# A DFT-and-GLU kernel: another order for the opening's loads, stores and first three steps

## Chip, cores, metric

The kernel runs on one core of one Trainium2 chip. Its time is the device time of one launch in microseconds (us); the median of three runs is compared. The profile is a hardware trace of one execution. The engines are TensorE (PE, with its weight loads as PEld), VectorE (DVE), ScalarE (ACT), GpSimd (POOL) and SyncE (SP), which here only issues DMAs. ScalarE and GpSimd issue some DMAs too, each on a queue of its own.

## What is computed

```python
X = np.fft.fft(x, axis=1)            # x: 8 x 3008 x 256, float32
X = np.fft.fft(X, axis=2)
h = X.real.reshape(24064, 256) @ w_in    # w_in: 256 x 2048
g = h * np.cos(h)
out = g @ w_out                      # w_out: 2048 x 256, out: 24064 x 256
```

All in float32. The output has 24,064 rows of 256.

## The kernel before

*The transform.* The sequence length is 3008 = 47 x 64. For each of the 8 batches, `first_half` multiplies the 47-point part: x lies in `xs[0]` and `xs[1]` (columns 0 to 15 and 16 to 31 of the 64, each with its mirror column), is folded along the feature axis by `fold` (sum and difference of mirrored features) and goes through TensorE in eight chunks of four columns to `z`. The result is evicted by ScalarE to tiles `zs`, stored to DRAM (`store_z`), and read back in another order (`load_z`). It is stored in two parts: "near" (far = 0, four of the 24 frequency rows, needed for the first group) and "far". `second_half` then multiplies the 64-point part with the table `BJ`, four rows at a time, which gives a group's `pq`. There are six groups (`NG`) of 225 or 256 columns in each batch.

*The weights.* The DFT over the feature axis is folded into w_in: `fold_weights(e, n)` multiplies a quarter n (512 columns) of w_in by the cosine (e = 0) or sine (e = 1) table into `WC` or `WS`. One row of the result, the norm row, is copied by VectorE to `nrow`, sent to DRAM (`send_wn`) and read back as columns `wn` (`take_wn`). `combine_w2(f0, f1)` makes four combinations of w_out's blocks on VectorE, four subtractions or additions for each call.

*The steps.* The body is a pipeline of 384 steps, eight for each group: `mm1` (two pairs of matmuls into PSUM tile `H`), a scaled copy `act_e`, `dve_h`, rounding (`act_round`, `dve_frac`), `act_sin`, `dve_g`, sums `dve_s`, and seven matmuls `mm2` three steps later (`LAG` = 3). Before `mm1`, `H` is filled: `seed` does it on ScalarE from the norm (tile `nb`) and `wn`; for step 0 `fill_first` and `seed_first` do it with a memset and two matmuls whose operand has one row. There are three `H` tiles.

*What sets the order.* The order is written out by hand (`tc.manual_schedule()`): every engine and every DMA queue takes its instructions in the order in which the Python code records them. DMA completions use eight counters shared by the SP and ScalarE queues; a DMA waits until the transfer that last used its counter has landed. The main loop over t records step t's parts; `opening` and `early` hang extra work on the steps 0 to 22, and `todo`, `aside` and `between` hang the next batch's transform on them.

*The opening.* LCS (DFT tables) and the first quarter of w_in come first on SP. Then the first half of x: its front part on SP in pieces of at most 2 KB, its mirrored part on ScalarE's queue, one mirror column (three small loads) on GpSimd's. The second half is all on SP. The second quarter of w_in and the first BJ columns follow. `chunk(c)` is fold(0, c, 0) and fold(0, c, 1). Chunk c + 1 is folded while TensorE multiplies chunk c:

```python
    for c in range(NCH):
        if c + 1 < NCH:
            chunk(c + 1)
        first_half(0, c)
        store_z(0, c, 0)
        if c == 3:
            load_w(2)
            load_w2(0, 4)
            send_wn(0)
    load_z(0, 0)
```

After it stand the near load of z, quarter 1's folds, one fold of quarter 2, six of the eight w2 blocks' combinations, the far z stores of the chunks 0 to 3 and `second_half(0, 0)`. Steps 0 to 2 go through the general loop, with `early` adding the remaining weight folds: one of quarter 2 in step 0, the two of quarter 3 in steps 1 and 2.

Of the kernel before, what the change touches and what calls it, by code (L numbers as in the profile page):

```python
# [18 lines left out]
ND = 256  # L19
NDFF = 2048  # L20
N2 = 47
NJ = 24
# [4 lines left out]
IP = 4  # L27
NCH = NI // IP
XP = 4 * IP
NG = 6  # L30
# [12 lines left out]
def _consts():  # L43
# [21 lines left out]
    LO0 = stack(np.sin(th), z, z, np.sin(thh))  # L65
    L = np.concatenate([LE, LO, LE0, LO0], axis=1)
    rows = np.zeros((128, 256))
    for side in range(2):
# [65 lines left out]
def kernel(  # L134
# [10 lines left out]
    LCS_dr = nc.inline_tensor(  # L145
        np.concatenate([L_np[:, 0:256], CS_np[0:128], CS_np[128:256]], axis=1), name="dft_L"
    )
    V_dr = nc.inline_tensor(np.ascontiguousarray(L_np[:, 256:640]), name="dft_V")
    ident_dr = nc.inline_tensor(np.eye(128, dtype=np.float32), name="ident")
# [38 lines left out]
    def load_x(b, p):  # L188
        xv = xs[p][0 : 16 * STEP].rearrange("(e g) c -> e g c", g=STEP)
        i0 = XP * p  # L190
        back = nc.sync if p else nc.scalar

        def load(queue, g, c0, c1, cols, **more):
            for m in range(3):
                k = 15 if m == 2 else 16
                queue.dma_start(
                    out=xv[0:k, g + m, ND * c0 : ND * c1].rearrange("e (i d) -> e i d", d=ND),
                    in_=x_r[b, 16 * m : 16 * m + k, cols],
                    **more,
                )  # L200

        load(nc.sync, 0, 0, XP, slice(i0, i0 + XP), max_dma_last_dim=2048)
        c0 = 0 if p else 1
        load(back, 3, c0, XP, slice(64 - i0 - c0, 64 - i0 - XP, -1))
        if p == 0:
            load(nc.gpsimd, 3, 0, 1, slice(32, 33))

    LCS = cpool.tile([128, 768], FP, tag="LCS", name="LCS")
    L = LCS[:, 0:256]
    CS = [LCS[:, 256 + 256 * i : 512 + 256 * i] for i in range(2)]  # L210
    wr = [
        spool.tile([128, n], FP, tag=tag, bufs=k, name="wr")
        for tag, n, k in (("mr", 1792, 1), ("cb", 1792, 1), ("r", 1024, 4), ("r", 1024, 4))
    ]
    BJ = cpool.tile([128, NJ * 128], FP, tag="BJ", name="BJ")
    w2 = cpool.tile([128, 16 * ND], FP, tag="w2", name="w2")

    def load_w(q):
        nc.sync.dma_start(
            out=wr[q][:, 0:1024].rearrange("p (i f) -> p i f", i=2),  # L220
            in_=moe_w_in.rearrange("(i p) f -> p i f", p=128)[:, :, 512 * q : 512 * q + 512],
        )

# [23 lines left out]
    nc.gpsimd.memset(xs[0][:, 2048:4096], 0.0)  # L247
    nc.vector.memset(VX[:, 0:512], 1.0)
    nc.vector.memset(ones, 1.0)
    nc.vector.memset(mask, 1.0)  # L250
    nc.vector.memset(mask[0:1], 0.0)
    nc.vector.memset(xs[1], 0.0)
    load_x(0, 0)
    for xf in xf0:
        nc.gpsimd.memset(xf[64:128], 0.0)
        nc.gpsimd.memset(xf[0:64, 512:1024:128], 0.0)
    load_x(0, 1)
    load_w(1)
    load_bj(0, 512)
    WC = cpool.tile([128, NDFF], FP, tag="WC", name="WC")  # L260
# [4 lines left out]
    xz = cpool.tile([128, ND], FP, tag="xz", name="xz")  # L265
    xs2 = [cpool.tile([128, 2 * ND], FP, tag=f"xs{e}", name="xs") for e in range(2)]
    xf1 = [cpool.tile([128, 512], FP, tag=f"xf{i}", name="xf") for i in range(2)]
# [14 lines left out]
    def fold(b, c, e):  # L282
# [3 lines left out]
        if e == 0:  # L286
            nc.gpsimd.tensor_copy(out=fv[:, 0, :, 0], in_=xv[:, :, 0])
        nc.vector.tensor_tensor(
# [120 lines left out]
    def first_half(b, c):  # L409

        if b:
            return first_half_later(b, c)
        if c % 4 == 0:
            middle(b, c // 4)
        fv = xf0[c % 2].rearrange("r (e c) -> r e c", e=2)
        LE, LO, LE0, LO0 = (L[:, 64 * q : 64 * q + 64] for q in range(4))
        pz = psum("pz", "M")
        a = 128 if c == 0 else 0
        for e, (w, w0) in enumerate(((LE, LE0), (LO, LO0))):
            rows = slice(64 * e, 64 * e + 64)  # L420
            if a:
                nc.tensor.matmul(
                    pz[rows, 0:128], lhsT=w0, rhs=fv[:, e, 0:128], start=True, stop=True
                )
# [12 lines left out]
    def store_z(b, c, far):  # L437
# [15 lines left out]
        for e in range(2):  # L453
            queue = nc.scalar if not far and (e or c > 3) else nc.sync
            queue.dma_start(
# [12 lines left out]
    def second_half(b, g):  # L468
# [16 lines left out]
        if g == 0:  # L485
            nc.scalar.copy(
                out=pv[:, :, 0:192].rearrange("d e (q k) -> d e q k", k=64), in_=bv[:, :, 1:4, :]
            )
            nc.scalar.copy(out=pv[:, :, 192:225], in_=bv[:, :, 0, 0:33])
        else:  # L490
# [10 lines left out]
    def spread_norm():  # L501
# [3 lines left out]
        nc.tensor.matmul(pn[:, 0:T], lhsT=ones, rhs=pq[0:1, T : 2 * T], start=True, stop=True)  # L505
        nc.scalar.copy(out=nb[:, 0:T], in_=pn[:, 0:T])

# [4 lines left out]
    def transform(b):  # L512
        t0 = (b - 1) * NG * 8

        def at(o, *call):
            todo.setdefault(t0 + o, []).append(call)

# [23 lines left out]
    def fold_weights(e, n, tag="M"):  # L541
        W = WS if e else WC
        pw = psum("pw", tag)
        for i in range(2):
            nc.tensor.matmul(  # L545
                pw,
                lhsT=CS[i][:, 128 * e : 128 * e + 128],
                rhs=wr[n][:, 512 * i : 512 * i + 512],
                start=(i == 0),
# [74 lines left out]
    def seed_first(s):  # L624
        T = s.T
        s.pq, s.nb = ready[s.b, s.grp]
        for u in range(2):
            nc.tensor.matmul(
                s.H[:, u * T : u * T + T],
                lhsT=nrow[0][0:1, 128 * u : 128 * u + 128],  # L630
                rhs=s.pq[0:1, T : 2 * T],
# [223 lines left out]

    keep_busy(1, "H", 512)
    fold_weights(1, 0, "H")
    fold_weights(0, 0, "H")
    chunk(0)
    for c in range(NCH):  # L860
        if c + 1 < NCH:
            chunk(c + 1)
        first_half(0, c)
        store_z(0, c, 0)
        if c == 3:
            load_w(2)
            load_w2(0, 4)
            send_wn(0)
    load_z(0, 0)
    load_w2(4, 8)  # L870
    take_wn(0)
    load_w(3)
    fill_first(steps[0])
    fold_weights(1, 1)
    fold_weights(0, 1)
    send_wn(1)
    load_bj(512, 1024)
    combine_w2(0, 2)
    combine_w2(2, 4)
    fold_weights(1, 2)  # L880
    take_wn(1)
    send_wn(2)
    combine_w2(4, 6)
    for c in range(NCH // 2):
        store_z(0, c, 1)
    second_half(0, 0)
    seed_first(steps[0])
    early = {0: (0, 2), 1: (1, 3), 2: (0, 3)}
    opening = {
        0: ((combine_w2, 6, 8), (take_wn, 2)) + tuple((store_z, 0, c, 1) for c in (4, 5)),  # L890
        1: ((send_wn, 3),) + tuple((store_z, 0, c, 1) for c in (6, 7)) + ((take_wn, 3),),
        2: ((clear_later,), (load_z, 0, 1), (load_bj, 1024, NJ * 128), (load_v,)),
        5: ((second_half, 0, 1),),
# [3 lines left out]
        22: ((second_half, 0, 5),),  # L897
    }
    n = len(steps)
    for b in range(1, NB):  # L900
        transform(b)

    def step(t, last=None):
# [11 lines left out]

    for t in range(n + LAG + 1):
        cur, prev, old, done = step(t), step(t - 1), step(t - 2), step(t - LAG)
        if cur:
            mm1(cur, 0)
            act_e(cur)  # L920
            if t == 0:
                spread_norm()
            if t in early:
                fold_weights(*early[t])
# [22 lines left out]
        for call in between.pop(t, ()):  # L947
            call[0](*call[1:])
        if done and t <= n:
            dve_s(done, 2)  # L950
# [56 lines left out]
```

## Time and profile before

| what | value |
|---|---|
| median of three runs (lowest, highest) | 1952.91 us (1952.51, 1953.36) |
| the profiled execution, its own time | 1953.48 us |
| its span, first to last instruction | 1951.7 us |
| granted TensorE clock, mean over the span | 0.994 |
| busy: PE, DVE, ACT, POOL | 1924.2, 1781.7, 1530.5, 396.0 us |
| moved by DMA | 89.32 MB, mean 46 GB/s |
| step 0's first matmul (L628) begins | 43.21 us |
| step 3's first matmul (L642) begins | 61.75 us |
| step 8's first matmul (L642) begins | 84.15 us |

A line such as "L642 PE MATMUL H<-pq,WC 128x225 x4" names the line of the code, the engine, the operation, the tile written and the tiles read, the size, and how many there were. One float32 matmul shows as two MATMUL records, so a pair of matmuls is x4. "[8.33 <-DMA w]" behind an instruction means that its engine had stood idle for 8.33 us, and that a DMA into tile w ended that. In the chain of waits every row is a start, a length and what the chain went through there; a DMA row ends when the data is in. "SPq" and "ACTq" are DMA issues. The granted clock is a share of TensorE's full clock.

### The profile page before, as it was taken

The page shows a single profiled execution, that of the slowest core. Times are in us where ns is not written, and L with a number is a line of the kernel's source. Part 1 is how long each engine was busy: PE and PEld are TensorE (multiplying, and loading weights), DVE is VectorE, ACT ScalarE, POOL GpSimd, SP SyncE. Part 2 cuts the span into 40 slices and gives each one's busy share as a digit, 9 for nine tenths or more (in the row PEclk, how much of TensorE's full clock was granted, in tenths as well). Part 3 has the DMA queues.
Part 4 walks back from the last instruction along what each step waited for, and adds up shares of the span by engine and source line. Part 5 has one row for each costly group of instructions (what it writes and reads, how often), then busy time and mean ns, then how long its engine had stood idle before and what let it go on. Part 6 is the DMA issues. An engine that isn't in the chain of part 4 may idle for free.

```text
span 1951.7 us, 30532 instructions
## 1 busy us (share of the span) xinstructions
PE 1924.2 (99%) x9524; PEld 1691.9 (87%) x9524; DVE 1781.7 (91%) x3343; ACT 1530.5 (78%) x2881; POOL 396.0 (20%) x464
## 2 busy tenths in 40 slices
PE   6999999999999999999999999999999999999998
PEld 3888889888998889988899888988889888898887
DVE  4889999999999998999989999899999999999998
ACT  2788878887788788887878888788877888788775
POOL 5022202222022211222112221122211222111101
PEclk8999999999999999999999999999999999999999
DMA  7321231012200122001211122110231100110000
GB/s 202 93 56 38 49 91 26 19 39 67 65 24 23 41 77 51 25 24 47 81 38 27 26 53 76 33 31 24 52 85 29 25 22 24 54 28 10 12 22 22
DMA packets 159969, 89.32 MB, mean 46 GB/s; under 512 B 108948, under 2 KB 153931, under 8 KB 157339
## 3 DMA queue, kind: packets, MB, share of 16 engines
q1 hardware_dynamic: 157135, 84.65, 16.7%
q0 software_dynamic: 1280, 1.68, 0.4%
q8 instruction: 76, 1.25, 0.3%
q10 hardware_dynamic: 1392, 1.05, 0.2%
q14 instruction: 86, 0.70, 0.1%
HBM read 50.04 MB, written 37.28 MB: 45 GB/s over the span
## 4 chain that ended last, share of the span: by engine, by line
PE 96%; DMA 1%; DVE 1%; issue 0%; ACT 0%; SPq 0%; ACTq 0%; POOL 0%; DVEq 0%; POOLq 0%
PE M L732 58%; PE H L642 34%; PE pb L475 2%; PE pz L382 2%; DMA zd<-zs 1%; DMA xp<-in_x_dram 1%; PE pz L342 0%; PE pw L545 0%; PE pz L425 0%; SPq L839 0%; PE M L382 0%; DVE r L687 0%; DMA z<-zd 0%; PE pz L370 0%; DVE S L698 0%
## 5 line engine op out<-in xcount | busy, mean ns | idle before, releaser
L732 PE MATMUL M<-S,VX 128*128 128x256 f32 (+1 forms) x2304 | 612.4, 375 | 0.0
L732 PEld LDWEIGHTS M<-S,VX 128*128 128x128 f32 x2304 | 437.8, 190 | 49.8
L673 ACT ACTIVATE r<-H 128x512 f32<-128x512 f32 (+1 forms) x384 | 226.1, 589 | 264.1 <-DVE h L658 263.3
L683 ACT ACTIVATE r<-r 128x1024 f32<-128x1024 f32 (+1 forms) x384 | 394.7, 1028 | 21.2 <-DVE r L677 16.1
L642 PE MATMUL H<-pq,WC 128*128 128x256 f32 (+1 forms) x1536 | 394.7, 379 | 1.9 <-ACT H L612 1.9
L642 PE MATMUL H<-pq,WS 128*128 128x256 f32 (+1 forms) x1536 | 387.8, 375 | 0.6 <-ACT ew L653 0.5
L732 PE MATMUL M<-r,w 128*128 128x256 f32 (+1 forms) x1536 | 387.7, 375 | 0.0
L612 ACT ACTIVATE H<-nb,wn 128x256 f32<-128x256 f32 (+1 forms) x766 | 363.0, 474 | 13.9
L658 DVE TENSOR_TENSOR h<-ew,H 128x512 f32<-128x512 f32 (+1 forms) x384 | 258.8, 674 | 103.3 <-PE H L642 72.4
L642 PEld LDWEIGHTS H<-pq,WC 128*128 128x128 f32 x1536 | 283.6, 190 | 52.5 <-ACT r L673 15.8
L732 PEld LDWEIGHTS M<-r,w 128*128 128x128 f32 x1536 | 300.3, 196 | 27.2
L642 PEld LDWEIGHTS H<-pq,WS 128*128 128x128 f32 x1536 | 291.7, 190 | 36.0 <-ACT ew L653 1.8
L677 DVE SCALAR_TENSOR_TENSOR r<-r,H 128x512 f32<-128x512 f32 (+1 forms) x384 | 258.6, 674 | 29.7 <-ACT r L673 13.0
L653 ACT ACTIVATE ew<-H 128x512 f32<-128x512 f32 (+1 forms) x384 | 225.7, 588 | 55.0 <-PE H L642 46.3
L784 POOL TENSOR_TENSOR cb<-cb,mr 128x256 f32<-128x256 f32 (+3 forms) x188 | 158.3, 852 | 517.8 <-DVE S L708 483.4
L698 DVE TENSOR_TENSOR S<-r 128x512 f32<-128x512 f32 (+1 forms) x384 | 258.8, 674 | 0.1
L677 DVE SCALAR_TENSOR_TENSOR r<-r,h 128x512 f32<-128x512 f32 (+1 forms) x384 | 258.4, 673 | 0.0
L687 DVE SCALAR_TENSOR_TENSOR r<-h,r 128x512 f32<-128x512 f32 (+1 forms) x384 | 258.0, 672 | 0.0
L687 DVE SCALAR_TENSOR_TENSOR r<-H,r 128x512 f32<-128x512 f32 (+1 forms) x384 | 255.9, 666 | 0.9 <-ACT r L683 0.5
L673 ACT ACTIVATE r<-h 128x512 f32<-128x512 f32 (+1 forms) x384 | 236.0, 615 | 0.0
L301 POOL TENSOR_TENSOR xs<-xp 113x512 f32<-113x512 f32 x112 | 143.1, 1278 | 440.9 <-DVE S L708 440.9
L732 PE MATMUL M<-S,w 128*128 128x256 f32 (+1 forms) x768 | 225.6, 375 | 0.6 <-DVE S L708 0.6
(94 smaller groups left out, 1579.7 us busy)
## 6 DMA issues: line engine op xcount, KB each, us to landing
out_dram<-ob SPq DMA_DIRECT2D x728, 32.0 KB
xp<-in_x_dram SPq DMA_DIRECT2D x250, 56.0 KB
z<-zd SPq DMA_DIRECT2D x8, 1280.0 KB
zd<-zs SPq DMA_DIRECT2D x224, 40.0 KB
nb<-nd SPq DMA_DIRECT2D x40, 128.0 KB
zd<-zs SPq DMA_DIRECT2D x224, 8.0 KB
xp<-in_x_dram SPq DMA_DIRECT2D x52, 48.0 KB
wr<-in_moe_w_in_dram SPq DMA_DIRECT2D x4, 512.0 KB
```

The lines of the kernel that those rows point to most:

```text
L301: return nc.gpsimd.tensor_tensor(out=xs2[e][0:XL], in0=xv[:, 0], in1=xv[:, 1], op=ALU.subtract if e else ALU.add,)
L612: nc.scalar.activation(out=s.H[:, u * T : u * T + T], in_=s.nb[:, 0:T], func=AF.Copy, bias=0.25, scale=wn[:, f : f + 1],)
L642: nc.tensor.matmul(s.H[:, u * T : u * T + T], lhsT=W[:, 128 * f : 128 * f + 128], rhs=s.pq[:, e * T : e * T + T], start=False, stop=True, ...
L653: nc.scalar.mul(out=s.ew[:, 0 : 2 * s.T], in_=s.H[:, 0 : 2 * s.T], mul=2.0)
L658: nc.vector.tensor_tensor(out=s.h[:, 0 : 2 * T].rearrange("p (u t) -> p u t", u=2)[:, :, ::-1], in0=s.ew[:, 0 : 2 * T].rearrange("p (u t) ...
L673: nc.scalar.activation(out=r, in_=h, func=AF.Copy, bias=BIG, scale=1.0)
L677: nc.vector.scalar_tensor_tensor(out=r, in0=r, scalar=-BIG, in1=h, op0=ALU.add, op1=ALU.subtract)
L683: nc.scalar.activation(out=r, in_=r, func=AF.Sin, bias=0.0, scale=SIN_SCALE)
L687: nc.vector.scalar_tensor_tensor(out=r, in0=h, scalar=-0.25, in1=r, op0=ALU.add, op1=ALU.mult)
L698: return nc.vector.tensor_tensor(out=sv[:, 0:2], in0=gv[:, 2:3].to_broadcast([128, 2, T]), in1=gv[:, 0:4:3], op=ALU.subtract,)
L732: nc.tensor.matmul(acc[key][m // 2][:, 256 * (m % 2) : 256 * (m % 2) + T], lhsT=w, rhs=a, start=first, stop=s.fp == 7, skip_group_check=True,)
L784: return nc.gpsimd.tensor_tensor(out=o, in0=a, in1=b, op=ALU.subtract if less else ALU.add)
```

## The change

It touches the opening only; the loop is the same from step 3 on, apart from what hangs on the steps 3 and 4.

- x of batch 0 is all on SP, first half and then second half, in pieces of 1 KB. The three small mirror loads stay with GpSimd. The clearing of `xs[1]` is split between VectorE and GpSimd.
- The loads of w_in are cut into two for each quarter; quarters 1 and 2, the first two w2 blocks and the first BJ columns are recorded right behind x, ahead of the z stores. Quarter 3 goes to the tiles `xs2`.
- The chunks go 0, 1, 2, 3, 7, 4, 5, 6. Chunk 7 (`DIRECT`) is not folded: TensorE takes x as it is, with two matmuls for each half, the second on reversed columns, and a table of negated sines (`NLO`) is added to LCS.
- The near z stores of the chunks 0 to 3 go to GpSimd's queue, one of each of the chunks 4 and 7 to SP, the rest to ScalarE. The column copy of `fold` goes from GpSimd to ScalarE. Two small copies (`edge` in `second_half`, `nb` in `spread_norm`) go from ScalarE to VectorE.
- The w2 blocks come in four loads, two of them right behind the near load of z. All far z stores and the far load are recorded ahead of step 0.
- Steps 0 to 2 are written out by hand in an order of their own, with step 1 seeded by matmuls as well; the folds of quarter 3 move to steps 3 and 4 and use another PSUM tile, and the combinations of the last two w2 blocks move there too.

```diff
-    L = np.concatenate([LE, LO, LE0, LO0], axis=1)
+    L = np.concatenate([LE, LO, LE0, LO0, -LO], axis=1)
...
-        load(nc.sync, 0, 0, XP, slice(i0, i0 + XP), max_dma_last_dim=2048)
+        load(nc.sync, 0, 0, XP, slice(i0, i0 + XP), max_dma_last_dim=1024)
         c0 = 0 if p else 1
-        load(back, 3, c0, XP, slice(64 - i0 - c0, 64 - i0 - XP, -1))
+        load(nc.sync, 3, c0, XP, slice(64 - i0 - c0, 64 - i0 - XP, -1))
...
+    xs2 = [cpool.tile([128, 2 * ND], FP, tag=f"xs{e}", name="xs") for e in range(2)]
+    wr.append(xs2)
...
+        for i in range(2):
+            nc.sync.dma_start(
+                out=wr[q][i],
+                in_=moe_w_in[128 * i : 128 * i + 128, 512 * q : 512 * q + 512],
+            )
...
+    nc.vector.memset(xs[1][:, 0:2048], 0.0)
+    nc.gpsimd.memset(xs[1][:, 2048:4096], 0.0)
...
-    nc.vector.memset(xs[1], 0.0)
...
     load_x(0, 1)
+    load_bj(0, 512)
     load_w(1)
-    load_bj(0, 512)
+    load_w2(0, 2)
+    load_w(2)
...
-            nc.gpsimd.tensor_copy(out=fv[:, 0, :, 0], in_=xv[:, :, 0])
+            nc.scalar.copy(out=fv[:, 0, :, 0], in_=xv[:, :, 0])
...
+            if c == DIRECT:
...
+                nc.tensor.matmul(
+                    pv[rows], lhsT=w[0:XR], rhs=xv[:, :, 0:128], start=True, stop=False
+                )
+                nc.tensor.matmul(
+                    pv[rows, :, 1:128],
+                    lhsT=(NLO if e else LE)[0:XR],
+                    rhs=xv[:, :, 255:128:-1],
+                    start=False,
+                    stop=True,
+                )
+                continue
...
-            queue = nc.scalar if not far and (e or c > 3) else nc.sync
+            queue = nc.sync if far or (e == 0 and c in (4, 7)) else nc.scalar
+            if c < 4 and not far:
+                queue = nc.gpsimd
...
-            nc.scalar.copy(out=pv[:, :, 192:225], in_=bv[:, :, 0, 0:33])
+            edge = nc.scalar.copy if b else nc.vector.tensor_copy
+            edge(out=pv[:, :, 192:225], in_=bv[:, :, 0, 0:33])
...
-        nc.scalar.copy(out=nb[:, 0:T], in_=pn[:, 0:T])
+        nc.vector.tensor_copy(out=nb[:, 0:T], in_=pn[:, 0:T])
...
-    keep_busy(1, "H", 512)
+    keep_busy(2, "H", 512)
...
+    order = [c for c in range(NCH) if c < 4] + [DIRECT] + [c for c in range(4, NCH) if c != DIRECT]
...
+    clear_later()
+    send_wn(0)
+    for s in steps[0:2]:
+        fill_first(s)
+    combine_w2(0, 2)
     fold_weights(1, 1)
     fold_weights(0, 1)
     send_wn(1)
+    load_z(0, 0)
     fold_weights(1, 2)
+    load_w2(2, 4)
+    load_w2(4, 6)
     take_wn(1)
     send_wn(2)
+    take_wn(0)
+    load_w(3)
+    load_w2(6, 8)
     for c in range(NCH // 2):
         store_z(0, c, 1)
+    take_wn(2)
+    for c in range(NCH // 2, NCH):
+        store_z(0, c, 1)
+    load_z(0, 1)
+    load_bj(512, 1024)
+    load_bj(1024, NJ * 128)
+    load_v()
+    combine_w2(2, 4)
+    combine_w2(4, 6)
     second_half(0, 0)
...
+        3: ((combine_w2, 6, 7), (send_wn, 3)),
+        4: ((combine_w2, 7, 8), (take_wn, 3)),
...
+    early = {3: (1, 3, "fft"), 4: (0, 3, "fft")}
...
+    s0, s1, s2 = steps[0:3]
+    seed_first(s0)
+    mm1(s0, 0)
+    act_e(s0)
+    spread_norm()
+    mm1(s0, 1)
+    seed(s2)
+    dve_h(s0)
+    act_round(s0, 0)
+    act_round(s0, 1)
+    seed_first(s1)
+    mm1(s1, 0)
+    act_e(s1)
+    dve_frac(s0, 0)
+    dve_frac(s0, 1)
+    mm1(s2, 0)
+    act_sin(s0)
+    mm1(s1, 1)
+    act_e(s2)
+    fold_weights(0, 2)
...
-    for t in range(n + LAG + 1):
+    for t in range(LAG, n + LAG + 1):
```

## The prediction

> **What bounds the kernel now.** First I read the page's slices of the span (40 equal slices, 48.8 us each; one digit is a busy share in tenths).
>
> ```profile
> PE   6999999999999999999999999999999999999998
> PEclk8999999999999999999999999999999999999999
> DMA  7321231012200122001211122110231100110000
> ```
>
> TensorE is full from the second slice on, at full clock. What the change touches can only move the moment at which that full stretch begins. So I cut the opening at the places where its character changes (columns: busy us of PE, PEld, DVE, ACT, POOL, then granted clock, DMA share, GB/s).
>
> ```profile
> 30.00:33.80 3.80, 3.80 (x10) 1.52 (x8) 0.00 (x0) 0.49 (x3) 1.94 (x4) 1.00 0.65 219
> 33.80:37.20 3.40, 0.37 (x1) 0.00 (x0) 2.72 (x8) 1.68 (x3) 3.40 (x11) 1.00 0.40 105
> 37.20:50.90 13.70, 9.77 (x22) 6.11 (x23) 2.93 (x8) 1.59 (x4) 6.98 (x13) 0.50 0.94 208
> 50.90:61.75 10.85, 8.43 (x30) 4.88 (x28) 7.01 (x14) 8.06 (x17) 0.00 (x0) 1.00 0.53 129
> 61.75:84.15 22.40, 22.36 (x119) 21.73 (x119) 21.13 (x45) 17.81 (x34) 0.69 (x1) 1.00 0.34 125
> ```
>
> From 61.75 (step 3's first matmul) TensorE and VectorE are both full: 22.36 and 21.13 of 22.40 us to step 8's first matmul at 84.15. Before that TensorE idles from 34 to 40 and then runs at half clock for 13.7 us. The chain of waits says what it waited for.
>
> ```profile
> 4.55 7.30 DMA xp<-in_x_dram
> ...
> 17.79 4.09 DMA xp<-in_x_dram
> ...
> 33.41 3.49 DMA zd<-zs
> 36.95 3.32 DMA z<-zd
> 40.31 2.09 PE pb L475 x8
> ...
> 43.21 1.86 PE H L628 x4
> ```
>
> x lands at 11.85 and 21.88, the last near z store at 36.95, z at 40.3; step 0's first matmul stands at 43.21. The order of time gives the prices that follow.
>
> ```profile
> 37.34 0.43 SPq L234 DMA_DIRECT2D w<-in_moe_w_out_dram  x1
> 45.00 1.87 PE L642 MATMUL H<-pq,WC 128*128 128x225 f32 x4
> 46.97 0.76 DVE L602 TENSOR_TENSOR VX<-w 128x256 f32<-128x256 f32 x2 [8.33 <-DMA w<-in_moe_w_out_dram]
> 47.84 3.45 PE L545 MATMUL pw<-wr,LCS 128*128 128x512 f32 x4
> 66.51 0.92 PE L642 MATMUL H<-pq,WC 128*128 128x225 f32 x4
> ```
>
> A pair of 225-column matmuls takes 1.87 us at half clock, 0.76 warm between starts; a weight fold (two 512-column matmuls) 3.45 and 1.72. The 1 MB of w2 asked for at 37.34 lands at 46.97, and VectorE stands 8.33 us for it; in before nothing urgent is queued behind that wait.
>
> **The change, part by part.** *x on one queue.* The second half of x began at 8.12, behind VectorE's 3.47 us memset, and its last part was issued at 17.79. Now the memset is split: VectorE ends at about 5.3, GpSimd at 4.35. The window of the first 10 us shows 230 GB/s, so 2.30 MB; the first half of x with all that stands ahead of it is 2.46 MB: 10.6 at the earliest. GpSimd's edge loads start 1.05 us later than before, and one took 5.9 us to land, so at the latest 12.9; I take 11.3, nearest to before's 11.85. The second half, 1.46 MB at about 0.3 MB/us: 16.2, against 21.88. The 1 KB pieces I cost at nothing: before's last x transfers have them and moved 340 GB/s between 20 and 22 us. A second warm-up matmul (0.86 us) delays weight fold 0 from 10.2 to about 11, just hidden by x; without that cover it would cost up to 0.9.
>
> *z.* Chunks 0 to 3 took 6.7 us (12.06 to 18.77): now to 18.1, and x is there. The unfolded chunk 7 has four matmuls where a folded chunk's two run side by side in 0.9: between 1.7 and 3.5; I take 2.6, since only the middle two touch different halves of the array. No row shows TensorE reading reversed columns; VectorE does it at its usual 0.69. ScalarE then sets the pace: per chunk 0.59 and 0.19 to evict, 0.3 per z store issued, and now some 0.25 for the column copy that GpSimd did. From 21.0 that is 1.1 + 0.25 + 1.1 + 0.25 + 1.4 + 1.1, the last store being issued at 25.9. It landed 3.5 us after issue in before (33.41 row); I take that: 29.4. Ends: 1.5 us (the first such store) and 7.0 (one in the thick of the weight loads), 27.4 to 32.9. The 1.84 MB of weights now ahead of z on SP are in by 16.2 + 1.84/0.35 = 21.5, hidden behind the chunks; if late, ScalarE's last stores wait, since they reuse those loads' completion counters. The eight stores moved to GpSimd (0.55 each, 4.4 us) lie beside this, and its b = 1 loads behind them are wanted only at step 7.
>
> *What moves on the queues.* SP takes three x parts from ScalarE's queue (0.6 us of issue each), eight w_in pieces for four and four w2 pieces for two (0.4 to 0.6 each), and gives the z stores of chunks 0 to 3 to GpSimd. Its order is now x, BJ, w(1), w2(0,2), w(2), two z stores, two norm rows, z, w2(2,4), w2(4,6). All that stands ahead of z is issued by about 15, as each waits for a transfer eight places earlier that has landed by then. The one send that could hold z back is the second norm row: TensorE folds quarter 1 from 24.6 to 26.3, ScalarE evicts by 27.0, VectorE copies by 27.7, and the send is out before 29.4. Cost nothing, with 1.7 us of cover.
>
> *The new wait.* z lands at 32.8, is multiplied by 34.9 and evicted at 35.4. But VectorE, which now copies the last 66 columns (0.22, before on ScalarE), has combine_w2(2,4) and (4,6) queued ahead, 1.66 us each, and these wait for w2 asked for right behind z. How late? The same bytes in before came 10.0 us after the z load's issue; 1.57 MB of the same kinds (w(2) and half of w2) issued at 24.63 were in about 6.5 us later, when the rate falls from 367 to 195 GB/s at 31.0; and 1.31 MB at that 0.37 MB/us, with 0.4 of issue and the 1.5 of the quickest z store, is 5.4. GpSimd's x loads run beside all three. I take 7.2, nearer to the middle row: 36.6. Then 1.66 + 0.22: step 0 starts at 38.5, not 43.21: −4.7.
>
> *Steps 0 to 2.* TensorE has idled, so they start at half clock. In series: seeds 1.86, first pair 1.87, norm row 1.1, second pair 1.87, step 1's seeds 1.86 and first pair 1.87: 10.4. Then I let it be warm (before was cold for 7.7 us after 43.21): 0.76 + 0.76 + 1.72 for step 2, step 1 and a fold, then on ScalarE 0.59 + 0.55 + 0.94 until step 3's H is seeded: 15.75 in all, where before took 18.54. −2.8; step 3 at 54.3, −7.5.
>
> *Steps 3 to 8.* Before had all four weight quarters folded by 61.75. Now the last quarter's fold is in steps 3 and 4: 2 x 1.72 = 3.44 on TensorE. VectorE's copy of its norm row (0.68) waits for ScalarE's eviction (0.69), with all of step 1's products queued behind it; and eight half-size combines (0.25 each) follow on an engine that has only 0.2 us of slack in a step of 4.19. Ends: 3.44 if VectorE's part lies beside, 6.3 if it adds. I take 4.6. Sum: −7.5 + 4.6 = **−2.9 us**. All else is off this path: the fourth quarter lands near 40; the 16 far z stores took 10 us (51.78 to 61.84), so the far z and BJ are in by about 56, wanted near 70; the last norm weights by 62, wanted near 67.
>
> The profiled execution took 1953.48 (span 1951.7), so 1950.6; the median is 0.57 below it: **1950.0**.
>
> [...] The clock fell to 0.50 at 37.2, 3 us after TensorE stopped, and came back at 50.9, 7.7 us after step 0 began. This speaks against the change: the wait for w2 makes a fresh idle stretch of 3.6 us (34.9 to 38.5) right before step 0. [...]
>
> **Rivals.** *Early clock* (13 in 100): the clock returns one short stretch after the seeds, at about 43.6 instead of 48.9. Of those 5.3 us, 3.1 are saved (0.76 for 1.87): −6.0, 1946.9. For it: 16.7 and 26.9, where it rose 4 us after TensorE started. Against: 43.21 to 50.9.
>
> *w2 early* (12): it lands 5.4 us after z's issue; step 0 at 36.7, −4.7, 1948.2; with the early clock as well −7.8, and with the cheap end of steps 3 to 8 −9.0, 1943.9. For it: 367 GB/s at 28 to 31 us. Against: the 8.33 us wait.
>
> *w2 late* (18), the one on the other side: 10 us as before, 39.4, seeds at 41.3. TensorE has idled 6.4 us and all of steps 0 to 2 is cold: 10.4 + 1.87 + 1.87 + 3.45 + 2.08 = 19.7. So −1.9 + 1.1 + 4.6 = +3.8, 1956.7. With the clock low throughout, the kernel is slower than before once w2 lands 1 us earlier than I take it or later (−2.9 + 3.95); with the clock as I take it, only from 39.5.
>
> *z no earlier than 32.9* (12): the last store takes 7 us, or ScalarE stands on a weight load's counter. All shifts by 3.5: +0.6, 1953.5.
>
> **How the numbers follow.** My forecast has 45 in 100, its own range 1947 to 1953. A measurement of this kernel tells about 0.2%, 3.9 us, from no change. Faster by more: the first two rivals and 17 of the 45: 42. Slower: 13 of the 18 of w2 late. The rest, 45, within. The range 1943.5 to 1956 leaves out the tails of both w2 cases.
>
> **What would show it.** Right: x in at 16 to 17, z's load issued by 30, VectorE idle before L625 until 35 to 38, step 3's matmul near 54, VectorE waiting at L581 in step 3. Wrong: z's load after 32, L625 not waiting, or the clock at 1.00 through steps 0 to 2.

## The result, and the profile after

| | median | lowest to highest |
|---|---|---|
| before, 17 runs | 1952.40 us | 1951.39 to 1953.88 |
| after, 17 runs | 1957.56 us | 1954.01 to 1959.26 |
| after / before | 1.0024 | 95% interval 1.0016 to 1.0031 |

The changed kernel is 0.24% slower, 5.2 us, where 2.9 us faster was forecast; 1957.56 lies outside the range of 1943.5 to 1956. The execution that was profiled with this result was the quickest of the 17 (span 1952.2, time 1954.01). The same kernel was profiled again, in an execution close to the median (span 1955.5), and "the second profile" below means that one. Between before's profile and this one lie 3.8 us; before's profiled execution was itself 1.1 us above its median (1953.48 against 1952.40), which is most of what is missing to 5.2.

In the slices of the span of the first profile TensorE's first slice has gained a tenth, some slices of the DMA engines differ by a tenth, and the rest is as in before (the granted clock too, not shown here).

```profile
PE   7999999999999999999999999999999999999998
DMA  8221131012200121101211122110231000110000
```

So the difference lies in the opening again. The second profile, cut where its character changes (columns as before: busy us of PE, PEld, DVE, ACT, POOL, granted clock, DMA share, GB/s):

```profile
26.65:30.45 3.80, 3.80 (x10) 1.54 (x9) 0.68 (x1) 1.27 (x2) 3.80 (x7) 1.00 0.40 107
30.45:34.09 3.64, 0.48 (x2) 0.00 (x0) 0.68 (x1) 0.69 (x1) 3.64 (x9) 0.88 0.77 215
34.09:43.41 9.32, 2.07 (x8) 1.78 (x8) 3.18 (x9) 0.48 (x1) 4.06 (x8) 0.50 1.11 202
43.41:60.55 17.14, 15.95 (x38) 10.84 (x38) 4.18 (x8) 6.27 (x13) 0.00 (x0) 0.60 0.74 224
60.55:87.98 27.43, 26.25 (x127) 23.12 (x127) 24.62 (x56) 19.44 (x37) 0.64 (x1) 1.00 0.12 43
```

z's load is issued at 30.45, against 36.95 before. But step 0's first matmul stands at 43.41, against 43.21: between z and the steps there are now 9.3 us in which TensorE works 2.07. Step 3 comes at 60.55 (61.75 before) and step 8 at 87.98 (84.15). The chain of waits goes where VectorE stood:

```profile
26.70 3.61 DMA zd<-zs
...
31.33 10.31 DMA w<-in_moe_w_out_dram
...
43.22 0.15 DVE pq L512
...
43.41 1.86 PE H L651 x4
```

And the order of time shows the wait itself (the bracket is the idle time ahead of the instruction and what ended it):

```profile
29.95 5.38 POOL L180 DMA_DIRECT2D xp<-in_x_dram  x10
30.45 0.35 SPq L486 DMA_DIRECT2D z<-zd  x1
...
36.10 0.76 DVE L625 TENSOR_TENSOR VX<-w 128x256 f32<-128x256 f32 x2 [3.73 <-DMA w<-in_moe_w_out_dram]
36.20 0.48 ACT L508 COPY pq<-pb 128x384 f32<-128x384 f32 x1 [4.54 <-PE pb L497]
...
41.67 0.76 DVE L625 TENSOR_TENSOR VX<-w 128x256 f32<-128x256 f32 x2 [4.01 <-DMA w<-in_moe_w_out_dram]
...
43.14 0.22 DVE L512 COPY pq<-pb 128x66 f32<-128x66 f32 x1
43.41 1.86 PE L651 MATMUL H<-pq,nrow 1*128 1x225 f32 x4 [7.25 <-DVE pq L512]
```

ScalarE has its part of `pq` at 36.7. The last 66 columns, 0.22 us of copying, stand on VectorE behind two calls of `combine_w2` (L625), of which the second waits until w2 lands at 41.67, and TensorE stands 7.25 us. In before the same copy was ScalarE's. The POOL row is the next batch's x, asked for by GpSimd in the same moments.

### The profile page after: what moved, and what is told of

It reads as the page before. It is cut to its first block, busy times and chain, and to the rows that moved or that the text cites. A ratio compares the mean times of both kernels' runs of the same rounds, so it can differ in the third digit from the quotient of the medians.

```text
span 1952.2 us, 30563 instructions
## 1 busy us (share of the span) xinstructions
PE 1927.7 (99%) x9534; PEld 1693.5 (87%) x9534; DVE 1780.4 (91%) x3348; ACT 1530.1 (78%) x2884; POOL 397.4 (20%) x465
## 4 chain that ended last, share of the span: by engine, by line
PE 96%; DVE 1%; DMA 1%; SPq 0%; issue 0%; ACT 0%; ACTq 0%; DVEq 0%
PE M L755 57%; PE H L665 34%; PE pb L497 2%; PE pz L387 2%; DMA w<-in_moe_w_out_dram 0%; PE pz L347 0%; DMA xp<-in_x_dram 0%; PE pz L445 0%; PE pw L568 0%; DVE r L710 0%; DVE S L721 0%; SPq L862 0%; PE H L651 0%; PE M L387 0%; SPq L195 0%
```

## The experiments

The marks of all profiles, in us from the span's start. "Last w2" is when the 1 MB of w2 asked for right behind z's load (two loads, in before and h1 one) was seen to be in, as a time after z's load was asked for. From step 8's start on all kernels need the same 1867.5 to 1868.0 us, so step 8 carries the whole difference. The medians of before that stood beside them were 1952.2 to 1952.6 us, and 1953.4 us for the h kernels, so the ratios are the thing to compare.

| kernel | z load | last w2 | seeds | step 3 | step 8 | median us | ratio, 95% interval |
|---|---|---|---|---|---|---|---|
| before | 36.95 | +10.0 | 43.21 | 61.75 | 84.15 | 1952.4 | 1 |
| after, quickest | 29.27 | +9.2 | 40.23 | 57.13 | 84.56 | 1957.6 | 1.0024 [1.0016, 1.0031] |
| after, again | 30.45 | +11.2 | 43.41 | 60.55 | 87.98 | 1957.4 | 1.0022 [1.0013, 1.0031] |
| e1 combines later | 31.03 | | 38.31 | 55.55 | 82.98 | 1951.8 | 0.9991 [0.9982, 1.0000] |
| e2 kept warm | 31.96 | +12.2 | 45.87 | 62.91 | 90.33 | 1956.5 | 1.0020 [1.0009, 1.0030] |
| e3 quarter 3 early | 31.18 | +13.5 | 46.41 | 62.84 | 87.77 | 1957.1 | 1.0019 [1.0009, 1.0028] |
| e4 = e1 + e3 | 30.73 | | 36.86 | 52.71 | 77.62 | 1947.0 | 0.9968 [0.9955, 0.9981] |
| f1 x held | 30.04 | +6.4 | 38.16 | 54.14 | 81.57 | 1951.3 | 0.9992 [0.9983, 1.0002] |
| f3 front alone | 32.30 | +10.2 | 37.91 | 57.22 | 79.62 | 1949.1 | 0.9981 [0.9972, 0.9990] |
| f4 mirrored x on ScalarE | 30.85 | +11.5 | 44.08 | 61.04 | 88.46 | 1957.7 | 1.0027 [1.0016, 1.0037] |
| g1 last combines early | 30.82 | +10.1 | 42.67 | 59.88 | 86.21 | 1956.8 | 1.0019 [1.0009, 1.0028] |
| g2 = e4 + f1 + g1 | 31.65 | +7.5 | 38.07 | 52.09 | 78.95 | 1947.2 | 0.9972 [0.9962, 0.9982] |
| g3 = g2, kept warm | 29.26 | +7.6 | 35.69 | 49.02 | 76.16 | 1945.3 | 0.9962 [0.9947, 0.9977] |
| g4 = f3, x held | 28.34 | +6.6 | 33.09 | 48.01 | 70.41 | 1941.5 | 0.9945 [0.9929, 0.9962] |
| h1 before, x held | 33.15 | +6.3 | 37.89 | 56.76 | 79.16 | 1948.5 | 0.9973 [0.9963, 0.9984] |
| h2 w2 ahead of z | 31.13 | no wait | 36.96 | 54.09 | 81.51 | 1951.5 | 0.9989 [0.9981, 0.9998] |
| h3 = e1, x held | 29.68 | +6.6 | 34.39 | 51.43 | 78.85 | 1947.9 | 0.9970 [0.9958, 0.9981] |

"Last w2" is read at VectorE's combination, and where that no longer waits for it (g2, g3, g4, h3) at GpSimd's read of w2, which may come a little after the landing. In e1 and e4 nothing waits for it, so it can't be read.

**The changed kernel again.** No edit.

> The changed kernel once more, to see which part of the opening differs between its executions (1954.0 to 1959.3 so far; the one profiled was the quickest). Theory A, the clock: steps 0 to 2 begin on an array that has idled, and the moment at which the granted clock returns to 1.00 differs; expected: the same landing times (x near 19, z's load issued near 29.3, w2 near 38.5, seeds near 40.2), but the clock back at 55 to 57 instead of 52, step 3's first matmul at 59 to 62 instead of 57.1, 1956 to 1959. Theory B, the loads: w2 itself lands later in the slower executions; expected: seeds at 42 to 45, the clock back about 12 us later as before.

Median 1957.43, as the first time. It gives the typical profile shown above, and that speaks for theory B: against the quickest execution z's load came 1.2 us later and w2 another 2.0, while steps 0 to 2 differ by 0.2 us (17.14 and 16.90).

**e1: the wait taken from ahead of the copy.** `combine_w2(2, 4)` goes behind step 0's `dve_frac`, `combine_w2(4, 6)` behind its `dve_g`:

```diff
     load_v()
-    combine_w2(2, 4)
-    combine_w2(4, 6)
     second_half(0, 0)
...
     dve_frac(s0, 1)
+    combine_w2(2, 4)
     mm1(s2, 0)
...
     dve_g(s0, 1)
+    combine_w2(4, 6)
     dve_h(s1)
```

> combine_w2(2,4) and (4,6) are recorded after step 0's fractions and products instead of ahead of the second half, so that the copy of the last 66 columns no longer stands behind w2. Theory B, the wait for w2: seeds at 35.4 instead of 40.2, all later work 4 to 5 us earlier, about 1952.5. Theory A, the clock: seeds at 35.4 too, but TensorE stays at half clock through steps 0 to 2, which then take 18 to 20 us instead of 16.9: 1953 to 1955, with a spread of 3 us or more. Rival: VectorE stalls inside step 0 on the same load (at 38.5), and nothing is won.

The order of time of e1: the copy now waits for ScalarE's part alone, and TensorE follows at once. VectorE waits for w2 nowhere any more.

```profile
37.52 0.48 ACT L508 COPY pq<-pb 128x384 f32<-128x384 f32 x1 [4.92 <-PE pb L497]
...
38.03 0.23 DVE L512 COPY pq<-pb 128x66 f32<-128x66 f32 x1 [4.71 <-ACT pq L508]
38.31 1.86 PE L651 MATMUL H<-pq,nrow 1*128 1x225 f32 x4 [0.83 <-DVE pq L512]
```

5.6 us between medians (1957.43 to 1951.82) for an edit that moves two calls. The seeds come at 38.31, not at the 35.4 expected: z's load was asked for at 31.03 and took 4.4 us to land. The wait behind w2 is what the change lost its head start to.

**e2: TensorE kept at work through the wait.** Eight products of 512 columns that nothing uses, two ahead of the z product, six behind it:

```diff
     combine_w2(4, 6)
+    keep_warm(2)
     second_half(0, 0)
+    keep_warm(6)
```

> Eight 512-column matmuls on the constant tables are added, two before and six after the second half of group 0, so that TensorE does not idle while it waits for z and w2; they compute nothing that is used. Theory A, the clock: granted 1.00 at the seeds, pairs of 225-column matmuls at 0.76 to 1.0 instead of 1.87, step 3's first matmul near 51 instead of 57.1; 1950 to 1952 and a spread under 2 us between executions. Theory B alone: no gain, since w2 lands no earlier: within 1 us of the changed kernel's quickest, 1954.

The windows of e2, cut at the end of the extra products (41.6), the seeds, step 3 and step 8:

```profile
35.00:41.60 6.60, 6.31 (x20) 3.09 (x20) 1.52 (x4) 0.48 (x1) 3.41 (x6) 1.00 1.08 236
41.60:45.87 4.27, 0.00 (x0) 0.00 (x0) 1.66 (x5) 0.00 (x0) 1.13 (x2) 0.99 1.10 196
45.87:62.91 17.04, 15.85 (x38) 10.82 (x38) 4.18 (x8) 6.28 (x13) 0.00 (x0) 0.60 0.74 244
```

Here w2 came 12.2 us after z's load, and TensorE stood 4.3 us once more. The clock was still full when it stopped, but it fell at 45.7, just ahead of the seeds, and steps 0 to 2 took 17.04 us, as cold as ever (17.14). So this run does not say what a warm start is worth; g3 does.

**e3: quarter 3's folds ahead of z.** `load_w(3)` behind `load_w(2)`, both folds behind `fold_weights(1, 2)`, and `early = {}`.

> Quarter 3 of w_in is loaded right behind quarter 2 and folded before the second half, not in steps 3 and 4. Theory C, the folds and the norm row's copy in steps 3 and 4 cost 5 us (57.1 to step 8 took 27.4 us against 22.4): step 3 to step 8 in 23 to 24 us, 3.5 to 4.5 us won. The folds also fill TensorE's wait for z, so the clock falls later. The near z stores lie behind 0.5 MB more on SP: z's load at 29.3 to 31. Together 1951 to 1954. Rival: the pipeline waits for VectorE's combines anyway and only the 1.7 us of slack on TensorE are won: 1955 to 1956.

Steps 3 to 8 took 24.93 us instead of 27.43: those folds are 2.5 of the 5.0 us. The time stayed (1957.1), neither the theory's figure nor the rival's: w2 came 13.5 us after z's load in the profiled execution.

**e4: e1 and e3 together.**

> The combines later and quarter 3 early together. If the wait for w2 (5.6 us in the run of e1) and the folds in steps 3 and 4 (2.5 of step 3 to 8 in the run of e3) are separate terms: 1949 to 1949.5. If e3's loss at the front (w2 landing 3 us later with 0.5 MB more ahead of z) stays: 1951 to 1952.

1947.0 us: without the wait, the 2.5 us of e3 come through, and steps 3 to 8 took 24.91 us again. It is 2 us better than the sum of the two (1949 to 1949.5). In the profiles z's product follows z's load sooner than in e1 (4.1 us, 4.4), and steps 0 to 2 took 15.85 us, not 17.23: quarter 3's folds fill TensorE's wait, and the clock falls only 1.4 us after the seeds began.

**f1: the next batch's x held.** Eight words of w2 are read by GpSimd, so that its 28 loads behind that read (1.46 MB) start when w2 is in; VectorE still waits as in the changed kernel.

```diff
+        if b == 1:
+            gate = cpool.tile([1, 8], FP, tag="gate", name="gate")
+            at(0, nc.gpsimd.tensor_copy, gate, w2[0:1, 2560:2568])
         for p, o in enumerate((0, 13) if b == 1 else (-20, -9)):
```

> GpSimd's 28 loads of the next batch's x (1.5 MB, issued from 22.6 on) are held until w2(4,6) has landed, by a copy of eight of its elements on GpSimd; nothing else moves. Theory D, contention: w2(4,6) takes 9 to 13 us from its issue because these loads share the DMA engines; expected then: w2 in 5.5 to 7 us, seeds at 37 to 38 instead of 40 to 46, 1952 to 1954. Rival, the queue itself: w2 still takes 9 us or more behind z and with w(3) and the rest behind it: 1956 to 1958.

The order of time of f1:

```profile
30.04 0.35 SPq L486 DMA_DIRECT2D z<-zd  x1
...
36.42 0.76 DVE L628 TENSOR_TENSOR VX<-w 128x256 f32<-128x256 f32 x2 [0.57 <-DMA w<-in_moe_w_out_dram]
36.45 0.44 POOL L976 COPY gate<-w 1x8 f32<-1x8 f32 x1 [13.68 <-DMA w<-in_moe_w_out_dram]
```

w2 is in 6.4 us after z's load, not 11.2, and VectorE's last wait is 0.57 us, not 4.01. Time 1951.3, 6.2 us less than after. The spread went too: 1950.4 to 1952.7, where the changed kernel ran from 1954.0 to 1959.3 (in h1 below, held as well, it did not go). It was these loads that made w2 late.

**f3: the front alone.** x, the chunks, z and its stores as changed; weights, combinations and steps 0 to 2 as in before, through the general loop (the changed kernel's order of these steps is called the own order below), and both small copies on ScalarE again:

```diff
-            edge = nc.scalar.copy if b else nc.vector.tensor_copy
+            edge = nc.scalar.copy
...
+    seed_first(steps[0])
+    early = {0: (0, 2), 1: (1, 3), 2: (0, 3)}
...
-    for t in range(LAG, n + LAG + 1):
+    for t in range(n + LAG + 1):
```

> The front of the changed kernel (x, weights, chunks, z stores) with steps 0 to 2, the evictions, the folds of quarter 3 and the far z stores of the kernel before. Theory B and C: the front brings z's load to 30 from 37, and what was lost came from the opening's second part; expected: z evicted at 36, seeds at 36 to 37, step 3 at 55 to 57, step 3 to 8 in 22.4 us as before: 1946 to 1949. Rival: the front's gain is used up by the wait for w2 in any order (VectorE's first product of step 0 stands behind combine_w2(4,6) here too): step 3 at 59 to 62, 1951 to 1954.

1949.1 us, 3.3 less than before. The seeds come 5.6 us after z's load, as nothing but z is waited for. But steps 0 to 2 need 19.31 us at a mean clock of 0.75, and w2 is 10.2 us behind z's load again.

**f4: the mirrored part of x's first half back on ScalarE's queue.**

> The mirrored part of the first half of x goes back to ScalarE's queue, all else as in the changed kernel. The first half of x landed at 12.7 to 13.7 in the changed kernel and its variants, 11.85 before. If the single queue is the cause: 11.9 again, z's load 1 us earlier; the end moves by 1 us or less, since w2 sets it: 1956 to 1957. If the 1 KB pieces or the order of the halves are: unchanged, 12.7 to 13.7, 1957 to 1958.

1957.7, no difference: one queue for x or two is not what decided. Nor did it bring x's first half back to before's 11.85 us: it was used from 14.2 here, from 13.2 in the second profile. Whether the 1 KB pieces or the order of the loads delay it was not tested.

**g1: the last combinations out of steps 3 and 4.** `combine_w2(6, 8)` stands behind step 0's second `dve_g` (the expectation says step 1's).

> The changed kernel with the combinations of the last two w2 blocks taken out of the steps 3 and 4 and made in one piece during step 1, after its second dve_g. Steps 3 to 8 took 27.4 us in the changed kernel, 22.4 before, and 24.9 where quarter 3's folds had been taken out of them. Theory: the other 2.5 us of the 5.0 are these eight half-size combinations on VectorE, which has 0.2 us of slack in a step. Then steps 3 to 8 take about 25 us, and the time falls by about 2.4 us to some 1955, unless the 1 MB of w2 asked for last has not landed by about 55 us, where VectorE would stand. Rival: the 2.5 us are the steps' own, because steps 0 to 2 leave step 3 with less done ahead of it than the general loop did. Then steps 3 to 8 stay above 26.5 us and the time stays at 1957.

Steps 3 to 8 took 26.33 us: 1.1 of the expected 2.5, and 0.6 us of time, within what can be told from nothing. My account of the second 2.5 us was too simple.

**g2: all three.**

> The changed kernel with three things put right at once: quarter 3's folds made ahead of z, all combinations of w2 that VectorE had ahead of its copy or in the steps 3 and 4 moved behind step 0's and step 1's dve_g and dve_h, and GpSimd's loads of the next batch's x held until the second 1 MB of w2 is in. The kernel with the first two of these took 1947.0 us, with steps 3 to 8 at 24.9. Theory: what stood in that kernel's way was w2's late landing, and the last combinations in steps 3 and 4; with both away, step 3's first matmul comes at 52 to 53 us, steps 3 to 8 take 22.4 to 23 us, and the time is 1943 to 1945.5. Rival: the three overlap, since TensorE at half clock is what steps 0 to 2 wait for in any case; then it is 1946 to 1948.

1947.2, the rival's figure: no better than e4 (1947.0). Steps 3 to 8 took 26.86. The two last combinations, now ahead of step 1's products, hold these up; TensorE stands 2.98 us for `act_e` behind them in step 3, and its clock then falls to 0.50 from 58.0 to 61.5. VectorE has this work to do somewhere, and in this order of steps there is no free place for it after z.

**g3: g2, kept warm.** One unused 512-column product after the z product, after each `seed_first` and after `spread_norm`.

> The kernel with all three put right, and with one unused 512-column product of TensorE after the z product and after each of three groups of one-row matmuls in steps 0 and 1. Theory of the clock: it falls, and stays low, because the one-row matmuls and the gaps between them do not count as work. Full-size products put between them then keep the clock at 1.00 from about 42 us on or earlier; each pair of 225-column products takes 0.76 to 1.2 us in place of 1.87 us, and step 3 comes 2 to 4 us earlier than without them, for 0.9 us each of products where TensorE waits anyway: 2 us faster than the kernel without them, if it was cold there. Rival: the clock stays at 0.50 for a fixed stretch all the same, and each of the four products costs up to 1.7 us at half clock: 1 to 4 us slower than the kernel without them.

Windows of g3, from the seeds to step 3 and to step 8:

```profile
35.69:49.02 13.33, 12.14 (x46) 7.75 (x45) 7.05 (x16) 6.17 (x13) 10.57 (x21) 1.00 0.68 197
49.02:76.16 27.14, 24.14 (x118) 23.03 (x119) 23.61 (x51) 17.89 (x34) 5.27 (x10) 0.94 0.53 136
```

Through steps 0 to 2 the clock does stay at 1.00, as the theory has it, and 13.33 us is the time of steps 0 to 2 in the own order when warm. g2, cold only from 41 to 48, took 14.02, so the extra products brought 0.7 us there, not 2 to 4. How much of the 1.9 us between the medians is theirs can't be said, since z's load came 2.4 us earlier in g3's profile. The 0.94 of the second window is again the 2.98 us wait in step 3, behind which the clock is at 0.50 from 55.4 to 58.8.

**g4: the front alone, x held.** f3 with f1's read.

> The new front alone (x, chunks, z and its stores as in the changed kernel, but weights, combinations and the steps 0 to 2 in the general loop as before), which took 1949.1 us, with GpSimd's loads of the next batch's x held until the second 1 MB of w2 is in. There w2's second 1 MB landed at 42.5, 10.2 us after z's load was asked for, and step 3 came at 57.2, 19.3 us after the seeds. Theory: VectorE's wait for this w2 in the combinations is what stretches steps 0 to 2; if it lands at 38 to 39, step 3 comes at 54 to 55 and the time is 1945.5 to 1947.5. Rival: the stretch is TensorE at half clock and the early weight folds; then the time stays at 1949.

The fastest kernel of the study: 1941.5 us, 0.9945 [0.9929, 0.9962], 4 us below what the theory gave. Its windows from z's load to the seeds, step 3 and step 8, and its order of time:

```profile
28.34:33.09 4.75, 3.75 (x15) 1.78 (x13) 2.36 (x6) 1.97 (x4) 0.00 (x0) 1.00 0.77 245
33.09:48.01 14.92, 12.50 (x42) 7.38 (x42) 10.29 (x23) 8.95 (x19) 12.27 (x23) 1.00 0.81 232
48.01:70.41 22.40, 22.35 (x118) 21.73 (x119) 21.13 (x45) 17.79 (x34) 4.07 (x8) 1.00 0.55 164
```

```profile
31.11 1.16 PE L497 MATMUL pb<-BJ,z 128*128 128x128 f32 x8 [0.18 <-DMA z<-zd]
...
33.09 1.02 PE L654 MATMUL H<-pq,nrow 1*128 1x225 f32 x4 [0.82 <-ACT pq L512]
```

z lands as TensorE ends the weight folds (0.18 us of idle time), and the clock does not fall in this execution: the seeds take 1.02 us, not 1.86. It was one of the two quicker of four (1940.2 and 1939.6 us, mean clock 0.998 and 0.999); the other two took 1942.8 and 1943.7 us at 0.996 and 0.997, so there the clock probably did fall. Holding x shortened the z path as well: its last store landed 1.4 us after the end of its issue, where f3 needed 3.6.

**h1: before, x held.** f1's read in the kernel before.

> The kernel before, with GpSimd's loads of the next batch's x held until its last 1 MB of w2 is in; nothing else changed. There that w2 lands 10.0 us after z's load is asked for, which was the upper of the three rows from which its landing in the changed kernel was estimated. Theory: the 10.0 us are those loads' doing. Then w2 lands 6 to 7.5 us after z's load, VectorE's wait of 8.33 us ends about 3 us earlier, and steps 0 to 2, which took 18.54 us, come to 15 to 17: the time is 1948.5 to 1950.5. Rival: w2 takes 10 us because it stands behind z and 0.5 MB of other weights on the same queue, whatever GpSimd does: 1952 as before.

```profile
33.15 0.34 SPq L464 DMA_DIRECT2D z<-zd  x1
...
39.42 0.76 DVE L605 TENSOR_TENSOR VX<-w 128x256 f32<-128x256 f32 x2 [2.91 <-DMA w<-in_moe_w_out_dram]
39.45 0.44 POOL L979 COPY gate<-w 1x8 f32<-1x8 f32 x1 [12.81 <-DMA w<-in_moe_w_out_dram]
```

In this order of time w2 is in 6.3 us after z's load, not 10.0: the same loads made the row from which the forecast's upper bound came. The time fell by 4.85 us, but not as I had it: z's load came 3.8 us earlier, since its last store was issued 2.1 us sooner and landed 1.7 us quicker, and steps 0 to 2 still took 18.87 us.

**h2: w2 ahead of z.** `load_w2(2, 4)` and `load_w2(4, 6)` behind `load_w(2)`; x is not held.

> The changed kernel with the two w2 loads that stand right behind z's load asked for ahead of it, right behind quarter 2 of w_in, at about 16 us; GpSimd's loads run as in the changed kernel. Between 22 and 30 us the DMA engines moved only 100 to 120 GB/s there. Theory: w2 was late because it was asked for at 30 us, beside z and the next batch's x. Then VectorE does not wait for it, step 0's seeds come right behind z's eviction, at 36 to 37.5 instead of 43.4, and the time is 1950 to 1952. Rival: the 1 MB now runs beside the near z stores and holds them up, so that z's load comes 2 to 3 us later, and the gain is no more than 3 us: 1953 to 1955.5.

1951.5: VectorE does not wait, the seeds come 5.8 us after z's load, and z's load, at 31.13, is not held up beyond the 29.3 to 32.3 of the other runs with the new front and GpSimd's loads beside it. From 22 to 30 us the DMA engines had moved 129 GB/s in the first profile of the changed kernel and 143 in the second, a little more than the expectation says. The place on the queue is as good a cure as holding x: w2 was late because it was asked for behind z, beside GpSimd's loads.

**h3: e1, x held.**

> The changed kernel with the combinations of w2 moved behind step 0's dve_frac and dve_g, so that VectorE's copy of the last 66 columns of pq waits for z alone, and with GpSimd's loads of the next batch's x held until w2 is in. The first edit alone gave 1951.8 us, the second alone 1951.3. Theory: both act on one wait, that of VectorE for w2 ahead of step 0. Then the second edit adds little to the first: seeds at 35 to 36.5, steps 0 to 2 16 to 17 us, steps 3 to 8 27.4: 1948 to 1950.5, still 7 to 9 us behind the new front with the general loop's steps 0 to 2 and the same hold (1941.5), which would then be the price of the own order of steps 0 to 4. Rival: with w2 and z on time TensorE does not idle long enough for its clock to fall, as in that kernel; then steps 0 to 2 take 12.5 to 14 us and the time is 1944.5 to 1947.

1947.9. The second edit did add to the first, some 4 us (0.9991 to 0.9970), because it also quickens z: the seeds come 4.7 us after z's load, and 7.3 in e1. But TensorE's clock fell all the same (z came 1.45 us after the folds, the copy later still), and steps 0 to 2 and 3 to 8 took 17.04 and 27.42.

One small turn that the prediction had at no cost: on SP's queue z's load stands behind the send of the second norm row, which waits for VectorE's copy. In h3 that send goes at 28.98 and z's load at 29.68; in g4, where the load is recorded ahead of it, the load goes at 28.34 with the same end of the last store's issue (26.97). The load follows the send by 0.7 us in f1, g2, g3 and the quickest execution of the changed kernel as well (28.58 and 29.27). In the second profile the z stores land later than this send (28.96 against 30.45), which hides it.

## Why the prediction was wrong

Term by term, with the second profile of the changed kernel:

| step of the forecast | forecast | found | difference |
|---|---|---|---|
| z's load issued | 29.4 | 30.45 | +1.05 |
| w2 in, after that | 7.2 | 11.22 | +4.0 |
| combination and copy, to the seeds | 1.88 | 1.74 | −0.1 |
| steps 0 to 2 | 15.75 | 17.14 | +1.4 |
| steps 3 to 8 above before's 22.40 | 4.6 | 5.03 | +0.4 |
| against before | −2.9 | +3.8 | +6.7 |

**The front came out within about 1 us, with terms that cancelled.** x was late: its first half was used from 13.2 (forecast 11.3), its second half from 19.1 to 19.5 (16.2), so that TensorE waited for it in chunk 7 and it stood on the chain, where "x is there" was forecast. Chunk 7 took 2.0 us, not 2.6, and ScalarE's evictions then set the pace as forecast: the issue of the last near store ended at 27.0 (it was forecast at 25.9), and it landed 3.6 us after it began (3.5). That z's load was only 1.05 us off is in part luck.

**The failed step is the landing of w2.** Three rows, 5.4, 6.5 and 10.0 us, were on the table, and I took 7.2, "nearer to the middle row". That row was not comparable: GpSimd's loads began 2.1 us into it (at 26.74), and the load in question has GpSimd's stream beside it from its start. With the stream running, eight profiles had 9.2 to 13.5 us; with it held, six had 6.3 to 7.6. Before's 10.0 was the one row with the same bytes in the same company, and h1 shows that it was company and not bytes. The sentence that VectorE waits for w2 ahead of its copy was right, and so was the price of each us of it: from w2's landing to the seeds the chain took 1.74 us (forecast 1.88), and when w2 landed at +6.4 (f1) the span was 2.5 us below before's, where the forecast for +7.2 was 2.9.

**w2 late was the rival that came true**, with +3.8 us at 18 in 100. That its figure is met exactly is partly luck: it had the seeds at 41.3 (found 43.41) and steps 0 to 2 all cold at 19.7 (found 17.14). The forecast's range ended at 1956, below this rival's own 1956.7. For the turning point the prediction had two figures: slower than before from w2 at 35.6 with the clock low throughout, and from 39.5 with the clock as I took it. It lies between them: with w2 at 36.42 (f1) the span was 2.5 us shorter than before's, with w2 at 38.48 (the quickest execution) 0.5 us longer.

**Steps 0 to 2: a borrowed clock.** I let the clock come back after the first 10.4 us of these steps, on the strength of the 7.7 us of before. In the second profile it came back 13.7 us after the seeds. In the general loop it was 7.6 to 9.7 us (before, f3, h1), in the own order 11.4 to 14.0, and 9.7 in g2, where it had fallen late. The fall came 2.3 us after TensorE stopped in the second profile and 4.1 us after in e2. For the rise it was not enough that TensorE showed as busy: in steps 0 to 2 of the second profile it shows 15.95 of 17.14 us, at half clock for 13.7 of them.

The traces say more on this. In them the granted clock changed only after whole stretches of 3.41 us: it was at 0.50 for 13.65 us, four of them, in before, and for 20.48 us, six, in the quickest execution of the changed kernel. Here are three such stretches of e3, one behind the other, counted from the fall of its clock:

```profile
51.88:55.30 3.42, 3.42 (x9) 2.16 (x9) 1.66 (x3) 1.62 (x4) 0.00 (x0) 0.50 0.39 89
55.30:58.71 3.41, 3.41 (x11) 3.06 (x10) 0.86 (x3) 1.94 (x3) 0.00 (x0) 0.50 0.94 369
58.71:62.12 3.41, 2.94 (x11) 1.64 (x9) 0.54 (x2) 1.19 (x3) 0.00 (x0) 1.00 1.00 404
```

TensorE is busy in all of the first and all of the second. The first holds 1.86 us of one-row products (step 1's seeds), the second nothing but 225-column pairs, and behind the second the clock is back. It is the same in the 14 profiles in which the clock was read through these steps and was low in them (all but g1, g3 and g4): of the stretches, counted likewise, that begin after the seeds' start, the clock came back at the end of the first with no more than 0.5 us of one-row products in it, and at the end of none with 0.7 us or more. That the one-row products are what kept it low is my estimate from these rows; no run has them alone. On that estimate the new order has a price: by seeding step 1 with matmuls as well, it has its last one-row product end 8.3 us after the seeds in the second profile, where before had it end after 4.7.

**Steps 3 to 8** cost 5.03 us in every kernel that kept them (27.42 to 27.45 against 22.40 in before, f3, g4 and h1). Quarter 3's folds are 2.5 of it (e3, e4). VectorE waits 2.1 us for ScalarE at L581 there, as forecast, as one row of VectorE's waits from 58 to 92 us in the second profile shows:

```profile
DVE nrow L581 <- ACT WS L577: 2.1, 1, 2.1
```

(Columns: us in total, times, longest.) How the other 2.5 us divide between VectorE's waits and the last combinations stays open: taking out the combinations brought 1.1.

**What the order of steps costs by itself.** From the seeds to step 8 the own order took 44.6 us in the changed kernel and 44.5 in h3, the general loop 41.7 (f3) and 41.3 (h1); with the clock up in steps 0 to 2, 40.5 (g3) and 37.3 (g4). The own order is some 3 us the worse in both pairs; in g3 the fall of the clock in step 3 is part of it. Against before's 40.9 that is +3.6, where I had −2.8 + 4.6 = +1.8. The front's 6.5 us, with which z's load came earlier, should have paid for it, and the wait for w2 took them.

## What to carry to other kernels

A landing time is read from a row with the same neighbours on the DMA engines, and only then from one with the same bytes: 1 MB took 11.2 or 6.4 us in the changed kernel and 10.0 or 6.3 in the kernel before, by whether another queue was loading beside it. Where an engine takes over a small copy on the path, look at what is recorded ahead of it there, since all of that now stands on the path too. Loads that are wanted much later can be held by one small read of the tile that is urgent: it was worth 4.9 us in the kernel before, 6.2 us in the changed kernel and 7.5 us with the new front alone. Keep one-row products few and early where TensorE starts at half clock: in e3 it showed as busy for all 3.42 us of a stretch with 1.86 us of them in it, and the clock came back only after the next stretch, which had none. That they are the cause is the estimate given above.

## What the runs showed of the hardware

- Beside GpSimd's loads of x a small store on ScalarE's queue landed later even while little was moved: from 26.65 to 30.45 us all DMA engines together moved 107 GB/s in the second profile, at a share of 0.40, where before had moved 340 GB/s between 20 and 22 us, and still z's load went only 3.5 us after the end of the issue of z's last store (3.6 in f3), against 1.4 us in g4, where these loads were held.
- The spread between executions does not go by these loads alone: 5.3 us among 17 runs of the changed kernel with them and 2.3 among 10 in f1 without, but 2.5 us among 17 runs of before with them and 5.8 among 8 in h1 without. In h1 and h3 the quickest run (1944.8 and 1946.2 us) has the highest mean clock, 0.998, where the slowest has 0.995.
- With the clock at 1.00, steps 0 to 2 took 4.4 us less in the general loop (19.31 in f3, 14.92 in g4) and 3.8 less in the own order (17.14 and, in g3, 13.33). Both pairs differ in more than the clock: in g4 w2 also came earlier, in g3 the folds and combinations stand elsewhere too.
- The granted clock changed only after whole stretches of 3.41 us: around step 0 it was at 0.50 for 6.8 us (g2) to 23.9 us (the second profile), two to seven stretches.
